# A fused gated layer with its backward pass on one core: sums of a short convolution moved to accumulating DMA, three more inverses in the wider form, forward products placed one step later

## The chip, the cores and the metric

The kernel runs on one core of a Trainium2 chip. The metric is the device time of one execution in microseconds; before the change the median of 3 runs is 1931.9 us (1931.69 to 1933.45). The profiled execution spans 1930.0 us, at a granted TensorE clock of 1.000.

## The reference, cut to what matters

The program computes one layer, its output and all its gradients (S = 2048 rows, D = 1024 channels, F = 3584, bf16):

```python
xn = layernorm(x)                                    # x: (S, D)
# A: a short convolution, a gate, a long convolution by FFT of length 2S
k_shift[s] = sum_t k[s - 3 + t] * shift_k[:, 3 - t]  # 4 taps, channel by channel
kv = k_shift * v
y  = irfft(rfft(kv, 2S) * rfft(ssm_k, 2S))[:S] + kv * ssm_D
s  = xn * y
# B: a bilinear gated unit
g  = silu(((xn @ w_gate) * (xn @ w_up)) @ w_down)
out = x + s * g
# and the gradients of x, k, v, shift_k, ssm_k, ssm_D, w_gate, w_up, w_down
```

## The kernel before, in words

The work runs in stages, and TensorE has matmuls in all of them. In the first, to about 521 us, xn is computed and multiplied with w_up and w_gate in 14 slabs of 256 columns. One unit of this (`gu_unit`) takes four blocks of 128 rows: 32 matmuls into PSUM tiles `psg` (line 661), ACT copies to `gut`, and one DVE multiply `hN` = gate x up, stored through the POOL queue (`Hd`), turned by TensorE some units later and stored as `HTd`. Then follow the product with w_down (`psbm`, line 985), the gates of the output, and the backward products (`psb`, `psx`).

The long convolution's forward half is a Python generator, `conv_forward`, that is pumped between the groups of `psg` matmuls: each `yield` gives the estimated cost of a step, and `tick` pulls steps so that the share of `F_TOTAL` that is done follows the share of the ticks that have passed. So the place of each step among the matmuls comes from these estimates. The DVE instructions of the generator, and the first matmul of each forward product, are pinned to this program order.

The 1024 channels are treated in eight slices (`ds`) of 128. For each slice there are two transforms, of the filter `h` together with `kv` pieces, into spectra KX and HX; then the product of the spectra; then an inverse transform. The steps, in order:

- `half` (lines 235 to 257): one half of a forward transform: 16 matmuls into two PSUM tiles `psF`, which ACT copies to an `SP` tile. There are two `SP` buffers and two `psF` buffers. Slices 0 and 7 use another form with eight residues (`EIGHT`).
- `transform`: the DVE sums of the two halves (`W<-SP`) and the outputs (`KX<-W`, `HX<-W`). At two places in it the function `ahead` issues the next half, or the turning of the next filter rows (`h_rows`).
- `product`: the spectra are multiplied on DVE, about 12 us.
- the inverse: `inv_dft` with four residues and four matmuls for each residue in the tail (`inv_rows`, line 449), or `inv8` with eight residues, more DVE work and two matmuls for each residue (`inv8_rows`, line 438). `INV8` says which slices take `inv8`: 2, 4 and 6. In the inverse the `kv` halves of the next slice are issued.

The short convolution (`shift`) makes `kv` for two slices (256 channels) at a time; `dp` counts these pairs. On DVE it is four products of `k` with a broadcast tap and three sums, all 128 x 4096 bf16, and a multiplication with `v`. `shift(0)` runs ahead of everything; those of `dp` 1, 2 and 3 (the "later shifts") run after the products of slices 1, 3 and 5. Their tiles are `krow` (k), `U[4]` (v), `U[6]` (the sum) and `U[7]` (the product of a tap). `load_kv` loads k and v for the next pair through the POOL queue; it is called at the start of slices 1, 3 and 5. `KFd`, `HFd`, `KSHd` and `YFd` are stores of the spectra, the shifted keys and the result, all on the POOL queue, which is in order.

The tiles `U[4]` to `U[7]` live in SBUF for the whole stage. After the last slice the generator ends, its PSUM is given back, and the `psbm` stage starts.

Of the kernel before, what the change touches and what calls it, by code (L numbers as in the profile page):

```python
# [13 lines left out]
BF16 = mybir.dt.bfloat16  # L14
# [5 lines left out]
def build_kernel(  # L20
# [11 lines left out]
    nc = tc.nc  # L32
    P = 128
# [3 lines left out]
    NB = S // P  # L37
# [206 lines left out]
    def net(w):  # L244
        w -= 0.95 * pe_us[0]
        pe_us[0] = 0.0
        return w
# [445 lines left out]

    h_out = []
    EIGHT = ((0, 0), (0, 1), (7, 0), (7, 1))
    INV8 = (2, 4, 6)
    SHIFT_W = 8 * 2.3

    conv_state = {"forward": True}
# [1 line left out]
    def conv_forward():  # L701
        S_ = conv_state

        def load_kv(dp, c):
            S_["k", dp] = krow
            if dp > 0 or c == 0:
                for i in range(2) if dp == 0 else (c,):
                    cld_k(krow[:, i], i, dp)
            if dp > 0 or c == 1:
                for i in range(2) if dp == 0 else (c,):  # L710
                    v = U[4][:, 2048 * i:2048 * i + 2048].rearrange("p (a x) -> p a x", a=8)
                    cld_v(v, i, dp * 256, 256)

        def load_h(ds):
            hrow = U[5][:, 0:2048].rearrange("p (c u r) -> p c u r", c=2, r=8)
            cld(U[5][:, 0:2048], A_ssm_k[ds * P:(ds + 1) * P, :])
            S_["h", ds] = hrow

        def shift(dp):
            kv = cx.tile([P, NB, 256], BF16, name="kv")  # L720
            S_["kvt", dp] = kv
            k = S_.pop(("k", dp))
            wb = lambda j: Wbc[:, j:j + 1, dp * 256:(dp + 1) * 256].unsqueeze(1).to_broadcast([P, 2, 8, 256])
            room = cx.tile([P, 16, 256], BF16, name="KX")[:].rearrange("p a x -> p (a x)") if dp == 0 else U[7][:]
            acc, prod, v = [t.rearrange("p (c r d) -> p c r d", c=2, r=8) for t in (U[6][:], room, U[4][:])]
            with tc.issue_after(last.ins):
                tt(acc, k[:, :, 0:8, :], wb(3), MUL)
            yield 2.3
            for j in (2, 1, 0):
                tt(prod, k[:, :, 3 - j:11 - j, :], wb(j), MUL)  # L730
                yield 2.3
                tt(acc, acc, prod, ADD)
                yield 2.3
            tt(kv[:].rearrange("p (c r) d -> p c r d", c=2), acc, v, MUL)
            st(KSHd[dp], U[6][:].rearrange("p (b d) -> p b d", b=NB))
            yield 2.3

        def h_rows(ds, c):
            if ds == 8:
                return  # L740
            hrow = S_["h", ds]
            if c == 0:
                S_["hx"] = cf.tile([P, NB, P], BF16, name="hx")
            pe_us[0] += 0.47
            ps = ps_tr.tile([P, 8, P], BF16, name="tr")
            with tc.issue_after(tr_ln[0].ins):
                nc.tensor.transpose(ps[:, 0, :], hrow[:, c, :, 0], ident[:])
            for r in range(1, 8):
                nc.tensor.transpose(ps[:, r, :], hrow[:, c, :, r], ident[:])
            nc.scalar.activation(S_["hx"][:, 8 * c:8 * c + 8, :], ps[:], ACT.Copy, scale=WSC)  # L750
            if c == 1:
                h_out.append(ds)
                if ds + 1 < 8:
                    load_h(ds + 1)

        def kvs(ds):
            return S_["kvt", ds // 2][:, :, ds % 2 * P:(ds % 2 + 1) * P]

        def tail(ds):
            G = S_.pop(("G", ds))  # L760
            yf = cs.tile([P, NB, P], BF16, name="yf")
            for rp in range(4):
                ps = (inv8_rows if ds in INV8 else inv_rows)(G, ps_y, rp)
                pe_us[0] += 0.45 if ds in INV8 else 0.9
                nc.scalar.copy(out=by_res(yf[:], rp), in_=rowps(ps))
                if rp == 3:
                    st(YFd[:, :, ds * P:(ds + 1) * P], yf[:])
                yield

        load_kv(0, 0)  # L770
        yield 0.0
        load_kv(0, 1)
        yield 0.0
        cx = pool("cx", 1)
        cs = pool("cs", 1)
        cf = pool("cf", 1)
        with tc.issue_after(xsts[3].ins):
            load_h(0)

        def half(ds, x, i, first=None):  # L780
            if (ds, int(first is not None)) not in EIGHT:
                return fwd4_half(x, i, cf, ps_cv, first)
            SP = cf.tile([P, 2, 2, 512], F32, name="SP", bufs=2)
            fwd8_half(x, i, SP, ps_cv, first, True)
            return SP

        def transform(ds, kind, sp, X, C, ahead, step):

            if (ds, kind) in EIGHT:
                W = fwd4_buf(cs)[:].rearrange("p a b c x -> p (a b c) x")  # L790
                for n, w in enumerate(fwd8(sp, X, W, C, ahead)):
                    if n in (0, 2, 4, 6):
                        step()
                    yield net(w)
                return
            W = fwd4_buf(cs)
            fwd4_sums(W, sp[0], 0)
            step()
            yield net(2.4)
            fwd4_sums(W, sp[1], 1)  # L800
            ahead(0)
            step()
            yield net(2.4)
            fwd4_outs(X, W, 0)
            ahead(1)
            step()
            yield net(2.4)
            fwd4_outs(X, W, 1)
            step()
            yield net(2.4)  # L810

        yield from shift(0)
        PIN[0] = True
        yield 3.9
        h_rows(0, 0)
        h_rows(0, 1)
        yield 0.1
        tl = turn_tables(ps_y)
        sp = [half(0, S_["hx"], i, Dz[:, 0:P]) for i in range(2)]
        for ds in range(8):  # L820
            yield 0.5
            if ds % 2 == 1 and ds < 7:
                with tc.issue_after(S_["kst"].ins):
                    for c in range(2):
                        load_kv(ds // 2 + 1, c)
            D0 = Dz[:, ds * P:(ds + 1) * P]
            sph = []
            KX = cx.tile([P, 16, 256], BF16, name="KX")
            HX = cs.tile([P, 16, 256], BF16, name="HX", bufs=2)
            own_room = lambda X: X[:].rearrange("p a x -> p (a x)").bitcast(F32).rearrange("p (a x) -> p a x", a=8)[:, 0:4]  # L830
            eight = (ds, 1) in EIGHT
            if ds == 0:
                yield from transform(0, 1, sp, HX, own_room(KX), lambda i: sph.append(half(0, kvs(0), i)), nop)
            else:
                yield from transform(ds, 0, sp, KX, own_room(HX), lambda i: sph.append(half(ds, S_["hx"], i, D0)), nop)
                S_["kst"] = st(KFd[ds], KX[:])
            next(tl, None)
            room = cf.tile([P, 4, 256], F32, name="room", tag="hx")[:] if eight else None
            yield from transform(ds, int(ds > 0), sph, HX if ds else KX, room, nop1 if eight else lambda c: h_rows(ds + 1, c),
                                 lambda: next(tl, None))  # L840
            if ds == 0:
                S_["kst"] = st(KFd[0], KX[:])
            if eight:
                h_rows(ds + 1, 0)
            turned(HX, 1, 0, 1)
            yield 1.3
            if eight:
                h_rows(ds + 1, 1)
            if ds == 7:
                cf.release()  # L850
                S_["forward"] = False
            st(HFd[ds], HX[:])
            yield from product(KX, HX, KX, cs, False, 0)
            if ds % 2 == 1 and ds < 7:
                yield from shift(ds // 2 + 1)
            sp = []

            def ahead():
                if ds < 7:
                    sp.append(half(ds + 1, kvs(ds + 1), len(sp)))  # L860
            yield from (inv8 if ds in INV8 else inv_dft)(KX, HX, cs, ahead if ds % 2 == 0 else None, ahead)
            if ds % 2 == 1:
                ahead()
            S_["G", ds] = HX
            tl = tail(ds)
        yield 6.0
        for _ in tl:
            yield 1.0
        cs.release()
        cx.release()  # L870
        kst.release()

    F_TOTAL = 4 * SHIFT_W + 6.0 + 8 * (0.5 + FWD4_W + 1.3 + PROD_W + INV_W) + 10.0 - 0.95 * 8 * (4 * 1.75 + 0.95 + 4 * 0.9)
    F_TOTAL += len(EIGHT) * (FWD8_W - 9.6 + 0.95 * 1.75) - 2.0
    F_TOTAL += len(INV8) * (INV8_W - INV_W + 0.95 * 1.8)
    conv = conv_forward()
# [771 lines left out]
```

## Time and profile before

| | PE | DVE | ACT | POOL | DMA share |
|---|---|---|---|---|---|
| whole span, 1930.0 us, busy us | 1913.8 | 1549.9 | 639.4 | 330.0 | |
| 120.7 to 480.4 us (slices 1 to 7), 359.7 us | 354.06 | 355.47 | 201.59 | 61.51 | 0.70 |
| 206 to 357 us, 151 us | 149.80 | 148.82 | 82.95 | 31.44 | 0.73 |
| 427 to 521 us, 94 us | 93.75 | 93.10 | 51.59 | 12.03 | 0.78 |

Each row is a stretch of the trace. A number is the time in which an engine had an instruction running. PE's ends are modelled, so its busy time says little of how densely it works; the start times of matmuls in the timeline are of more use. The DMA share is the mean share of the 16 DMA engines' time in which they had packets. A wait names the engine that waited, and the instruction that released it. The DMA table gives the time from issue to landing.

### The profile page before, as it was taken

How to read it: one execution, taken by the hardware profiler on the slowest of the kernel's cores; microseconds unless marked ns; L12 is line 12 of the kernel's file. 1: busy time of each engine (PE TensorE's matmuls, PEld its weight loads, DVE VectorE, ACT ScalarE, POOL GpSimd, SP SyncE). 2: the span in 40 equal slices, each digit the busy share in tenths (PEclk: the TensorE clock that was granted, in tenths of full speed). 3: DMA queues.
4: the chain of work that ended last, by engine and by line, in shares of the span. 5: the costliest groups of instructions: out<-in, count | busy, mean ns of one | idle time of the engine just before them, and what ended most of it. 6: DMA issues, size and time to landing. Idle time of an engine off the chain costs nothing.

```text
span 1930.0 us, 27487 instructions
## 1 busy us (share of the span) xinstructions
PE 1913.8 (99%) x10978; PEld 1030.2 (53%) x10978; DVE 1549.9 (80%) x1730; ACT 639.4 (33%) x942; POOL 330.0 (17%) x461
## 2 busy tenths in 40 slices
PE   8999999999999999999999999999999999999999
PEld 5555555555544457666666666664444444444444
DVE  9999999999937556888899999999996403388883
ACT  5764555555423234333222222221222102011113
POOL 4121212111112220000122132021111101111111
PEclk9999999999999999999999999999999999999999
DMA  8876766667889987666788788575797999889883
GB/s 292 268 259 217 254 211 228 225 199 265 283 252 316 310 284 264 211 206 207 262 247 262 243 238 269 195 268 186 219 258 172 141 215 218 163 179 193 194 204 130
DMA packets 451360, 444.43 MB, mean 230 GB/s; under 512 B 268800, under 2 KB 371612, under 8 KB 436768
## 3 DMA queue, kind: packets, MB, share of 16 engines
q1 hardware_dynamic: 394848, 243.36, 47.6%
q0 software_dynamic: 40064, 169.95, 27.3%
q10 hardware_dynamic: 16320, 29.36, 4.1%
q8 instruction: 86, 1.41, 0.3%
q14 instruction: 42, 0.34, 0.1%
HBM read 194.00 MB, written 185.64 MB: 197 GB/s over the span
## 4 chain that ended last, share of the span: by engine, by line
PE 85%; DVE 9%; issue 2%; DMA 2%; ACT 1%; SPq 0%; POOL 0%; ACTq 0%; DVEq 0%; POOLq 0%
PE psb L1356 20%; PE psx L1486 20%; PE psb L1339 10%; PE psbm L985 10%; PE psg L661 10%; PE psb L1434 9%; DVE W L213 2%; PE psF L235 2%; DVE HX L213 1%; DVE KX L213 1%; DVE U L213 1%; PE psY L438 1%; DMA HTd<-hT 1%; PE psY L1132 1%; DVE bst L561 1%
## 5 line engine op out<-in xcount | busy, mean ns | idle before, releaser
L661 PE MATMUL psg<-wslab,U 128*128 128x512 bf16 x1792 | 407.3, 379 | 2.9 <-DMA wslab<-in_B_w_gate_dram 0.9
L1356 PE MATMUL psb<-U,U 128*128 128x512 bf16 x1792 | 397.0, 379 | 0.0
L1486 PE MATMUL psx<-U,dgut 128*128 128x512 bf16 x1536 | 332.8, 379 | 0.0
L1486 PEld LDWEIGHTS <-dgut 128*128 128x128 bf16 x1792 | 175.3, 98 | 211.4
L1356 PEld LDWEIGHTS <-U 128*128 128x128 bf16 x1792 | 175.3, 98 | 197.9
L661 PEld LDWEIGHTS <-U 128*128 128x128 bf16 x1792 | 172.6, 98 | 188.9 <-issue 2.1
L1339 PE MATMUL psb<-wdt,U 128*128 128x256 bf16 x1792 | 205.6, 273 | 0.0
L1339 PEld LDWEIGHTS <-U 128*128 128x128 bf16 x1792 | 175.2, 98 | 29.2
L1434 PE MATMUL psb<-U,U 128*128 128x512 bf16 x816 | 177.1, 379 | 0.0
L213 DVE TENSOR_TENSOR W<-W 128x1024 f32<-128x1024 f32 (+1 forms) x174 | 171.6, 1003 | 3.7
L1361 ACT CAST wb<-psb 128x512 bf16<-128x512 f32 x112 | 65.6, 586 | 315.1 <-PE psb L1356 304.7
L985 PE MATMUL psbm<-U,ht 128*128 128x512 bf16 x672 | 145.7, 379 | 0.0
L1434 PEld LDWEIGHTS <-U 128*128 128x128 bf16 x896 | 87.4, 98 | 104.5
L663 ACT CAST gut<-psg 128x512 bf16<-128x512 f32 x156 | 91.5, 587 | 127.8 <-PE psg L661 127.0
L1518 ACT ACTIVATE dx_t<-dxn 128x1024 bf16<-128x1024 f32 x15 | 15.9, 1058 | 324.9 <-DVE dxn L213 321.0
L985 PEld LDWEIGHTS <-ht 128*128 128x128 bf16 x672 | 65.6, 98 | 78.6
L213 DVE TENSOR_TENSOR U<-U,dht 128x2048 bf16<-128x2048 bf16 x56 | 68.3, 1221 | 46.9 <-ACT dht L1341 46.9
L1184 DVE SCALAR_TENSOR_TENSOR dkp<-dkT,kT 128x1024 bf16<-128x1024 bf16 (+2 forms) x64 | 78.4, 1224 | 33.3 <-DMA dkT<-DKSHd 31.5
L1341 ACT CAST dht<-psb 128x512 bf16<-128x512 f32 x112 | 65.7, 587 | 116.3 <-PE psb L1339 116.3
L213 DVE TENSOR_TENSOR dxn<-psx,dxna_t 128x1024 f32<-128x1024 f32 x15 | 18.3, 1222 | 83.3 <-PE psx L1486 79.2
L66 POOL DMA_DIRECT2D Hd<-hN x54 | 37.0, 685 | 265.7 <-DVE hN L213 263.9
L1465 ACT CAST wbs<-psb 128x512 bf16<-128x512 f32 x51 | 29.9, 586 | 146.5 <-PE psb L1434 134.2
(260 smaller groups left out, 2462.8 us busy)
## 6 DMA issues: line engine op xcount, KB each, us to landing
U<-GUd SPq DMA_DIRECT2D x28, 1024.0 KB, 7.7
DGd<-U SPq DMA_DIRECT2D x28, 1024.0 KB, 5.9
GUd<-gut ACTq DMA_DIRECT2D x39, 512.0 KB, 5.1
out_dram<-wb SPq DMA_DIRECT2D x112, 128.0 KB, 4.1
U<-Hd SPq DMA_DIRECT2D x14, 1024.0 KB, 5.9
Hd<-hN POOLq DMA_DIRECT2D x54, 256.0 KB, 4.5
HTd<-hT SPq DMA_DIRECT2D x52, 256.0 KB, 3.7
ht<-HTd SPq DMA_DIRECT2D x6, 1536.0 KB, 10.1
```

What stands on the lines that cost most here:

```text
L213: pinned(V.tensor_tensor(o, a, b, op))
L235: mm = nc.tensor.matmul(ps[:, k].rearrange("p (c d) -> p c d", c=2), T[:, r, k, :], xr[:, r], start=(n == 0), stop=(n == len(rs) - 1 and ( ...
L661: gu_mm[0] = nc.tensor.matmul(ps[:], XNT[q][:, dc, qi * P:(qi + 1) * P], w[:, dc].rearrange("p a f -> p (a f)"), start=(dc == 0), stop=(dc ...
L663: nc.scalar.copy(out=gut[:, :, i], in_=ps[:].rearrange("p (a f) -> p a f", a=2))
L985: mm = nc.tensor.matmul(ps[:, dh * 512:(dh + 1) * 512], ht(fc)[:, i * P:(i + 1) * P], WD[fc // 4][:, fc % 4, dh * 512:(dh + 1) * 512], sta ...
L1184: ins = V.scalar_tensor_tensor(prod[:].rearrange("p r d -> p (r d)")[:, lo:H], dkT[:, 0, lo:H], 1.0, kT[:, 0, 13 + m + lo:13 + m + H], op0 ...
L1339: nc.tensor.matmul(ps[:, x * SLW:(x + 1) * SLW], DBMT[2 * hf + g][:, dc, (b % 4) * P:(b % 4 + 1) * P], wdt[:, dc, :], start=(dc == 0), sto ...
L1341: nc.scalar.copy(out=dht[:, 2 * e:2 * e + 2].rearrange("p b f -> p (b f)"), in_=ps[:])
L1356: nc.tensor.matmul(ps[:], XN[b // 4][:, b % 4, dc * P:(dc + 1) * P], dgus[b // 8][:, :, b % 8], start=(b == 0), stop=(b == NB - 1))
L1361: nc.scalar.copy(out=wb[:, dc % 2].rearrange("p a f -> p (a f)"), in_=ps[:])
L1434: nc.tensor.matmul(ps, h[:, f, b, :], DBM[b // 4][:, b % 4, dh * 512:(dh + 1) * 512], start=(b == 0), stop=(b == NB - 1))
L1486: nc.tensor.matmul(ps[:, dh * 512:(dh + 1) * 512], t[n][:, f, i * P:(i + 1) * P], WGU[n][:, f, dh * 512:(dh + 1) * 512], start=(n == 0 and ...
```

## The change

It has four parts.

1. The three sums of each later shift are no longer DVE instructions. `shift_parts` computes the product of a tap on DVE into `U[7]`, and an accumulating DMA on the POOL queue adds it to `U[6]`. As the product tile is used again, each product must wait until the DMA before has landed; so the three parts are spread over the slice: two products ahead of the first transform, one after it, one after the second transform, and the multiplication with v after the product of the spectra. `shift(0)` stays as it was.
2. `INV8` takes in slices 1, 3 and 5, so six inverses use the form with eight residues.
3. In `transform` (the form of slices 1 to 6) both calls of `ahead` come one step later.
4. The loads of k and v for the next pair are issued at the end of the even slice before, since the first product is now needed at the start of the odd slice. `F_TOTAL` is adapted to the new sum of costs.

It is for taking work off DVE and spending it on inverses that need fewer matmuls, and for giving the forward products more distance from the sums that free their buffers.

```diff
-    INV8 = (2, 4, 6)
+    INV8 = (1, 2, 3, 4, 5, 6)
...
+        def shift_parts(dp):
+            k = S_.pop(("k", dp))
+            wb = lambda j: Wbc[:, j:j + 1, dp * 256:(dp + 1) * 256].unsqueeze(1).to_broadcast([P, 2, 8, 256])
+            rows = lambda t: t.rearrange("p (c r d) -> p c r d", c=2, r=8)
+            acc, prod, v = rows(U[6][:]), rows(U[7][:]), rows(U[4][:])
+            def part(j):
+                tt(prod, k[:, :, 3 - j:11 - j, :], wb(j), MUL)
+                pinned_add = nc.gpsimd.dma_start(out=U[6][:], in_=U[7][:], accum_op=ADD, max_dma_last_dim=4096)
+                return pinned_add
+            tt(acc, k[:, :, 0:8, :], wb(3), MUL)
+            yield 2.3
+            part(2)
+            yield 2.3
+            yield None
+            for j in (1, 0):
+                part(j)
+                yield 2.3
+                yield None
+            kv = cx.tile([P, NB, 256], BF16, name="kv")
+            S_["kvt", dp] = kv
+            tt(kv[:].rearrange("p (c r) d -> p c r d", c=2), acc, v, MUL)
+            st(KSHd[dp], U[6][:].rearrange("p (b d) -> p b d", b=NB))
+            yield 2.3
...
             fwd4_sums(W, sp[1], 1)
+            step()
+            yield net(2.4)
+            fwd4_outs(X, W, 0)
             ahead(0)
             step()
             yield net(2.4)
-            fwd4_outs(X, W, 0)
+            fwd4_outs(X, W, 1)
             ahead(1)
-            step()
-            yield net(2.4)
-            fwd4_outs(X, W, 1)
             step()
             yield net(2.4)
...
+            sh = iter(())
             if ds % 2 == 1 and ds < 7:
-                with tc.issue_after(S_["kst"].ins):
-                    for c in range(2):
-                        load_kv(ds // 2 + 1, c)
+                sh = shift_parts(ds // 2 + 1)
+            def some():
+                for w in sh:
+                    if w is None:
+                        return
+                    yield w
+            yield from some()
...
                 S_["kst"] = st(KFd[ds], KX[:])
+                yield from some()
...
             st(HFd[ds], HX[:])
+            yield from some()
             yield from product(KX, HX, KX, cs, False, 0)
-            if ds % 2 == 1 and ds < 7:
-                yield from shift(ds // 2 + 1)
+            yield from some()
+            if ds % 2 == 0 and ds < 6:
+                with tc.issue_after(S_["kst"].ins):
+                    for c in range(2):
+                        load_kv(ds // 2 + 1, c)
...
-    F_TOTAL = 4 * SHIFT_W + 6.0 + 8 * (0.5 + FWD4_W + 1.3 + PROD_W + INV_W) + ...
+    F_TOTAL = SHIFT_W + 3 * 5 * 2.3 + 6.0 + 8 * (0.5 + FWD4_W + 1.3 + PROD_W + INV_W) + ...
```

More of the change, by code (lines that the diff above doesn't have):

```diff
@@ L871, in conv_forward @@
         kst.release()
-    F_TOTAL = 4 * SHIFT_W + 6.0 + 8 * (0.5 + FWD4_W + 1.3 + PROD_W + INV_W) + 10.0 - 0.95 * 8 * (4 * 1.75 + 0.95 + 4 * 0.9)
+    F_TOTAL = SHIFT_W + 3 * 5 * 2.3 + 6.0 + 8 * (0.5 + FWD4_W + 1.3 + PROD_W + INV_W) + 10.0 - 0.95 * 8 * (4 * 1.75 + 0.95 + 4 * 0.9)
     F_TOTAL += len(EIGHT) * (FWD8_W - 9.6 + 0.95 * 1.75) - 2.0
```

## The prediction

> **What bounds the kernel now.** I read the stage table (40 windows), then the waits of each engine between 90 and 530 us, then the timelines of DVE, PE and ACT there, because the change touches only the forward stage, which ends near 530 us. Two rows of the stage table, each: window, length, then busy us (instructions) of PE, weight loads, DVE, ACT and POOL, granted clock, DMA share, GB/s:
>
> ```profile
> 386.00:434.25 48.25, 47.44 (x296) 26.68 (x295) 47.84 (x36) 26.43 (x37) 5.20 (x8) 1.00 0.60 199
> 530.75:579.00 48.25, 48.25 (x241) 23.41 (x240) 14.61 (x24) 12.80 (x14) 6.21 (x9) 1.00 0.87 251
> ```
>
> In the forward stage DVE and TensorE are both full at 99%; from 530 us on TensorE is full and DVE has room. TensorE then stays full until about 1880 us, so what the forward stage saves or loses on TensorE moves the end one to one. The page's "99% PE" does not say which of the two sets the pace here; the waits and the timelines do. Waits of PE (first line) and of DVE (the others) from 90 to 530 us, in us in total, times, longest:
>
> ```profile
> PE psF L235 <- ACT SP L257: 4.9, 4, 2.5
> DVE hN L213 <- ACT gut L663: 0.8, 1, 0.8
> DVE W L213 <- ACT gut L663: 0.5, 1, 0.5
> ```
>
> Each engine waits for the other a little: TensorE waits 4.9 us in four places, DVE 1.3 us in two. One of the four places, on PE, ACT and DVE (start, length):
>
> ```profile
> 426.36 1.95 PE L235 MATMUL psF<-hx,TF 128*128 128x256 bf16 x16 [0.80 <-ACT SP L257]
> 425.29 1.93 ACT L257 COPY SP<-psF 128x1024 f32<-128x1024 f32 x2 [1.10 <-DVE W L213]
> 422.82 4.63 DVE L213 TENSOR_TENSOR W<-SP 128x1024 f32<-128x1024 f32 x4
> ```
>
> A forward product (psF) needs its PSUM buffer, which the ACT copy of the half before empties, which needs an SP buffer (two of them), which the DVE sums of two halves earlier free. So the second half can start only about 1.1 us after the DVE sums of three halves earlier. DVE has no gap around there. These products, last at 479.3 us, are where a late DVE stops TensorE; after the last one nothing in DVE holds TensorE.
>
> **What the skill says.** (1) "Collectives: The Full Stack", section "The bandwidth ceiling: the fold count and why AG ≠ RS ≠ AR": an adding transfer is slower than a copy because it reads two sources for each write, not because of the add; reduce-scatter measured 32.35 GB/s against 62.28, on two engines, so some 16 GB/s for one engine. The trace has no accumulating DMA, so no run here shows it yet. (2) "DMA: Bandwidth & Descriptors", section "SWDGE vs HWDGE vs iDMA": accumulation goes through GpSimd's queue only. So the new transfers stand in the queue with the KFd, HFd and Hd stores. (3) "SBUF — State Buffer", "Who interferes with whom": a tensor_tensor with both inputs in SBUF contends with GpSimd's reads, and (an inference, it says) not with descriptor writing. The trace agrees: POOL issues a 1 MB KFd store in 557 ns while DVE is 99% busy.
>
> **The change, part by part.**
>
> *TensorE work.* Inverses 1, 3 and 5 go from four matmuls for each residue to two: 16 fewer each, 48 in all. Eight such matmuls take 0.87 us start to start (431.17 to 432.04 in the timeline), 0.109 us each: 5.2 us less TensorE work.
>
> *DVE work.* Rows by shape (busy us, mean ns):
>
> ```profile
> L213 DVE TENSOR_TENSOR U<-U,U 128x4096 bf16<-128x4096 bf16 x9 | 20.6, 2289 | 0.2
> L213 DVE TENSOR_TENSOR U<-k,Wbc 128x4096 bf16<-128x4096 bf16 x12 | 27.3, 2286 | 0.1
> ```
>
> The nine sums U<-U,U go to the DMA. Start to start such an instruction costs 2.27 us (a whole shift from 165.08 to 184.40 less two hN multiplies of 0.60: 18.1 us for eight), so 20.4 us go. The three wider inverses cost more: an eight-residue inverse takes 456.03 to 473.07 less two hN, 15.8 us; a four-residue one 412.84 to 422.82 less one hN, 9.4; 6.4 more each, 19.3 in all. Net about -1 us; counted instruction by instruction at the last forward product it is -0.7. So the DVE work is traded, not reduced; only TensorE gets lighter.
>
> *Forward products one step later, new total of the pump.* Nothing is added; it changes where the products stand among the gate matmuls. I counted, in both built orders, TensorE work and DVE work ahead of every half. For the last half (filter product of slice 7, second half) 1624 gate matmuls stand before it, then 1627. TensorE work ahead of it falls by 4.5 us, that behind it by only 0.7. For the same half of slice 6 the split is 0.9 ahead and 4.3 behind.
>
> *Loads of k and v one step earlier.* Their place in the POOL order for the first of them (slice 1) does not change: the second block of k is issued at 124.69 us and its 704 KB take 8.7 us, landing at 133.4. The first product of the shift now stands ahead of slice 1's transform, where DVE arrives at 131.8 us. That is a new DVE wait of 1.6 us. For slices 3 and 5 an eight-residue inverse lies between, and the loads land well ahead: nothing.
>
> *The nine accumulating DMAs.* New waits of DVE: the next product overwrites U7, so it waits until the DMA has read it, and the last multiply waits for U6. Queued behind a waiting DVE instruction is everything on DVE in order: transform sums (TensorE's products wait for these), hN multiplies. The room for each is what DVE does between, from slice 1 of the trace before: KX transform with one hN 131.80 to 141.07 plus 0.6, 9.9 us; HX transform and turn 141.07 to 152.09, 11.0; product with two hN 152.09 to 165.08, 13.0. For the duration, plain 1 MB stores of the same queue land so (KB each, median us):
>
> ```profile
> KFd<-KX POOLq DMA_DIRECT2D x8, 1024.0 KB, 4.6
> HFd<-HX POOLq DMA_DIRECT2D x8, 1024.0 KB, 5.9
> KSHd<-U POOLq DMA_DIRECT2D x3, 1024.0 KB, 5.2
> ```
>
> From below: about 2 us of fixed time (the Trainium skill, "DMA: Bandwidth & Descriptors", section "Anatomy of one DMA — SWDGE (gpsimd) path") and 1.05 MB at 16 engines x 16 GB/s, 4.1 us, is 6.1 us, an estimate from the collectives figures. From above: moving twice, in engines that are already 0.55 to 0.95 busy in these windows, and behind a KFd or HFd store issued 2.3 us ahead: with what that store still needs (up to 3.6 us) and twice the movement of a slow HFd (8.2 us landing, so twice 6.2), some 14 to 16 us. I take 7 for the first, 9 for the second (2.3 us behind KFd), 10 for the third: all below 9.9, 11.0 and 13.0, so no stall. The spread keeps both ends.
>
> *Sum.* The end follows DVE's path to the last forward product. DVE reaches the sums that free it 0.7 us earlier by work, 1.2 earlier because its waits on gut go (TensorE is ahead now); the half had 2.8 us of slack before (479.3 against 475.4 + 1.1); the TensorE work behind it is 0.7 less. Together 5.4 us, less the 1.6 us of the k load: 3.8. 1931.9 - 3.8 = 1928.1. The same sum at slice 6's half gives 4.3 + 0.7 + 0.7 + 1.2 = 6.9 less 1.6, so it doesn't bind. I say 1928.0.
>
> **The rivals.**
> A, TensorE alone sets the pace: the later products leave enough slack that a late DVE is never seen. Then all 5.2 us and the 4.9 us of waits go: about 1921.8. For it: only four waits. Against: DVE is 99% busy and its work is not less.
> B, slower: the accumulations become the bound. At 12 us each the stalls are 2.1 + 1.0 + 0 per slice, 9.3 over three: 1937.4. At 15 us 5.1 + 4.0 + 2.0, 33 in all: 1961. For it: DMA share 0.94 in the window 152 to 165 of the trace and an unmeasured operation. Against: the estimate of 6 to 10 us.
> C, the accumulations cost about what is won: 10.5 to 11.5 us each, some 0.6 to 2.1 us per slice, 2 to 6 in all: 1930 to 1934.
>
> **How the numbers follow.** The forecast (1926 to 1929.5) 0.40, A 0.15, C 0.22, B 0.23. Faster by over 0.2% is below 1928.04: A whole, and some two thirds of the forecast, since the k wait may be partly hidden: 0.15 + 0.28 = 0.43. Slower is above 1935.76: B but for its mildest part and none of C, 0.22. The rest, 0.35, is no change. Range 1922.5 (A's region nearly whole) to 1941 (the milder half of B): some 0.07 below and 0.12 above left out.
>
> **What would show it.** PE's waits on SP between 90 and 530 us near 3 to 5 us still, not 0 (A). DVE waits on k of about 1.6 us near 132 us. DVE waits on the U DMA of under 1 us each in nine places; over 2 us shows B. The accumulating DMA's landing in the DMA table: 7 to 10 us. The first psbm matmul (520.97 us before) near 517. The prediction is wrong if the accumulations land later than 11 us, if ACT's hT copies start to wait for HTd stores (0.2 us before) because the DMA engines are fuller, or if the stages after 530 us change at all.

## The result, and the profile after

The changed kernel takes 1940.12 us (median of 4 runs, 1939.49 to 1940.28), the kernel before 1931.98 (4 runs); the ratio is 1.004, 95% interval 1.0023 to 1.0057. It is some 8 us slower, where 4 us less were forecast. The profiled execution spans 1938.2 us.

The stage table again, for the same two stretches; the columns are those of before (window, length, then busy us and instructions of PE, weight loads, DVE, ACT and POOL, granted clock, DMA share, GB/s):

```profile
386.00:434.25 48.25, 42.94 (x236) 21.98 (x239) 43.51 (x41) 21.00 (x31) 7.52 (x10) 0.93 0.86 263
530.75:579.00 48.25, 47.96 (x247) 23.81 (x251) 21.08 (x27) 13.80 (x16) 4.76 (x7) 1.00 0.86 246
```

In the forward stage TensorE lost 4.5 us of 48 and DVE 4.3, the granted clock fell to 0.93, and the DMA share rose from 0.60 to 0.86. From 530 us on TensorE is as full as before (all of that stage lies 8.2 us later, so the window holds a little other work). The first `psbm` matmul starts at 529.16 us (520.97 before), and from there to the end both kernels take 1409.0 us, so the whole loss, 8.2 us, is there when the forward stage ends.

What is as planned shows in the rows by shape of DVE and in the DMA table (KB each, median us to landing). No sum `U<-U,U` of this shape is left, the nine accumulating DMAs have taken their place, and only the waits ahead of the rows are new (x13 counts the whole execution, with one product of the first shift):

```profile
L213 DVE TENSOR_TENSOR U<-k,Wbc 128x4096 bf16<-128x4096 bf16 x13 | 29.6, 2287 | 1.6 <-DMA k<-in_A_k_dram 1.6
L213 DVE TENSOR_TENSOR kv<-U,U 128x4096 bf16<-128x4096 bf16 x4 | 9.2, 2292 | 6.9 <-DMA U<-U 6.9
```

```profile
HTd<-hT SPq DMA_DIRECT2D x52, 256.0 KB, 4.1
U<-U POOLq DMA_DIRECT2D x9, 1024.0 KB, 9.8
HFd<-HX POOLq DMA_DIRECT2D x8, 1024.0 KB, 7.8
```

The median landing of 9.8 us lies in the forecast 7 to 10, but it hides two kinds. By slice (1, 3, 5) the first accumulation took 8.0, 8.4 and 8.5 us, the second 9.8, 10.0 and 8.7, the third 14.2, 15.3 and 15.1.

The waits from 90 to 545 us, in us in total, times, longest: PE, then DVE, then ACT (its ordinary waits on PE and DVE left out).

```profile
PE psg L661 <- ACT gut L663: 9.2, 2, 4.9
PE psF L235 <- ACT SP L257: 2.0, 1, 2.0
...
DVE kv L213 <- DMA U<-U: 6.9, 3, 2.7
DVE W L213 <- ACT SP L257: 2.7, 2, 1.7
DVE U L213 <- DMA k<-in_A_k_dram: 1.6, 1, 1.6
...
ACT hT L691 <- DMA HTd<-hT: 14.7, 3, 6.6
```

Three of these are new and large. DVE waits 6.9 us for the third accumulations; ACT waits 14.7 us for `HTd` stores (0.2 before); TensorE waits 9.2 us for ACT in two places, where it waited for none of ACT's `gut` copies before. The timelines of the second place, of SP's queue, ACT and PE (start, length, instruction, idle time before it and its releaser), show how the last two hang together:

```profile
387.42 0.37 SPq L540 DMA_DIRECT2D wslab<-in_B_w_up_dram  x1
387.84 1.89 SPq L540 DMA_DIRECT2D wslab<-in_B_w_gate_dram  x1
392.40 21.77 SPq L61 DMA_DIRECT2D HTd<-hT  x3
...
412.78 1.01 ACT L691 COPY hT<-tr 128x1024 bf16<-128x1024 bf16 x1 [6.61 <-DMA HTd<-hT]
413.69 1.08 ACT L663 CAST gut<-psg 128x512 bf16<-128x512 f32 x2
...
407.77 1.67 PE L661 MATMUL psg<-wslab,U 128*128 128x512 bf16 x7
414.33 2.29 PE L661 MATMUL psg<-wslab,U 128*128 128x512 bf16 x5 [4.88 <-ACT gut L663]
```

The slab loads issued at 387 us land only after 11.8 and 24.2 us. The `HTd` store of 392.40 stands behind them in SP's queue and lands after 20.3. There are two `hT` buffers and a copy into one of them every 7.35 us (391.36 and 398.71 us), so a store that takes more than some 13.6 us (two such steps less the copy of 1.0) holds up a copy: the next copy `hT<-tr` on ACT waits until 412.7; the `gut` casts stand behind it in ACT's order; and TensorE, out of `psg` buffers, idles for 4.88 us. The other place is the same at 298.30 us (4.28 us idle). The Trainium skill ("DMA: Bandwidth & Descriptors", section "Queues, rings and completion order") says that SP's queue has one ring on each engine and that each engine takes the descriptors of a ring in order; the store that lands 0.6 us after the slab load ahead of it (412.7 and 412.1) agrees.

The idle time has a tail. The columns of these windows are those of the stage table:

```profile
142.00:146.00 4.00, 4.00 (x20) 2.48 (x20) 4.00 (x4) 2.73 (x3) 0.00 (x0) 0.57 1.02 195
...
406.00:410.00 4.00, 3.45 (x16) 1.47 (x15) 2.22 (x3) 0.17 (x1) 0.00 (x0) 1.00 1.05 248
410.00:414.00 4.00, 0.00 (x0) 0.00 (x0) 3.23 (x2) 1.22 (x2) 1.25 (x2) 0.76 1.08 418
414.00:418.00 4.00, 3.45 (x8) 1.28 (x9) 3.93 (x4) 0.83 (x3) 0.00 (x0) 0.50 0.94 362
418.00:422.00 4.00, 4.00 (x30) 2.60 (x29) 3.97 (x6) 2.29 (x4) 0.69 (x1) 0.89 0.21 73
```

After the idle 4.88 us the granted clock is 0.50 for some 4 us and 0.89 in the 4 after: 4 x 0.50 + 4 x 0.11, 2.4 us of TensorE time more. The Trainium skill ("TensorE: Matmul & The Clock Gate", section "Part 1: The HAM clock gate") gives the clock as halved after an idle window of some 3.4 us and restored after as long a busy one; both stalls, of 4.28 and 4.88 us, agree. But here a shorter gap did it too: the 2.0 us that a `psF` product waits at 140 us are followed by a clock of 0.57 from 142 to 146 us, 1.7 us more, while the longest `psF` wait before the change, 2.5 us, left the clock at 1.00. So the two stalls take 4.3 + 4.9 + 2 x 2.4, about 14 us, from TensorE in this execution; how much of this reaches the end the experiments had to tell. The DMA share is over 1 (the times of packets overlap) from 406 to 414, up to the landings, and 0.21 after.

### The profile page after: what moved, and what is told of

Read it like the earlier page. It is cut to its first block, busy times and chain, and to the rows that moved or that the text cites. A ratio compares the mean times of both kernels' runs of the same rounds, so it can differ in the third digit from the quotient of the medians.

```text
span 1938.2 us, 27286 instructions
## 1 busy us (share of the span) xinstructions
PE 1906.9 (98%) x10796; PEld 1027.8 (53%) x10930; DVE 1547.1 (80%) x1751; ACT 637.8 (33%) x942; POOL 341.8 (18%) x470
## 4 chain that ended last, share of the span: by engine, by line
PE 83%; DVE 5%; issue 3%; DMA 3%; ACT 1%; POOL 1%; POOLq 0%; ACTq 0%; DVEq 0%
PE psb L1393 20%; PE psx L1523 20%; PE psb L1376 10%; PE psbm L1022 10%; PE psb L1471 9%; PE psg L661 8%; DMA HTd<-hT 2%; DVE W L213 2%; PE psF L235 2%; PE psY L438 1%; DVE KX L213 1%; PE psY L1169 1%; DMA U<-U 1%; PE psx L1471 1%; DVE m L213 1%
## 5 line engine op out<-in xcount | busy, mean ns | idle before, releaser
L213 DVE TENSOR_TENSOR W<-W 128x1024 f32<-128x1024 f32 (+1 forms) x192 | 190.1, 1007 | 4.1
```

The source lines that it names most:

```text
L213: pinned(V.tensor_tensor(o, a, b, op))
```

## The experiments

My theory after this reading: the intended parts are worth about what was forecast, and two losses eat it, the waits for the third accumulation on DVE's path and the `HTd` stall on TensorE's. The rivals: that the later products or the wider inverses cost the time; that the size of the packets, not the amount of data, delays the other transfers. All ratios, to the kernel before run beside each (they are not quotients of two medians; where kernels of different experiments are compared below, it is by these ratios):

| kernel | us | ratio | 95% interval |
|---|---|---|---|
| after | 1940.12 | 1.0040 | 1.0023 to 1.0057 |
| e1 copies in place of sums | 1930.07 | 0.9988 | 0.9981 to 0.9994 |
| e2 third sum on DVE | 1936.56 | 1.0025 | 1.0017 to 1.0034 |
| e3 inverses as before | 1945.91 | 1.0069 | 1.0054 to 1.0084 |
| e4 forward products as before | 1941.44 | 1.0051 | 1.0033 to 1.0070 |
| e5 HTd stores on ACT's queue | 1936.08 | 1.0018 | 1.0004 to 1.0033 |
| e6 smaller packets | 1948.44 | 1.0090 | 1.0074 to 1.0105 |
| e7 all nine sums on DVE | 1947.31 | 1.0079 | 1.0064 to 1.0094 |
| e9 three mends | 1930.57 | 0.9986 | 0.9975 to 0.9998 |
| e10 three mends, five wide inverses | 1928.02 | 0.9975 | 0.9968 to 0.9982 |
| e11 kv multiply later | 1938.70 | 1.0037 | 1.0022 to 1.0052 |
| e12 before, products one step later | 1931.21 | 0.9997 | 0.9981 to 1.0013 |
| e13 e5 and e11 together | 1929.68 | 0.9987 | 0.9979 to 0.9995 |
| e14 three mends, four wide inverses | 1932.48 | 1.0004 | 0.9996 to 1.0012 |

### e1: the change without the adding

```diff
-  nc.gpsimd.dma_start(out=U[6][:], in_=U[7][:], accum_op=ADD, max_dma_last_dim=4096)
+  nc.gpsimd.dma_start(out=U[6][:], in_=U[7][:], max_dma_last_dim=4096)
```

The transfers stay, with their order and waits, but copy instead of adding; the later shifts' sums are left out.

> The nine accumulating DMAs become plain copies of the same megabyte at the same places; the sums of the later shifts are left out, so k_shift is wrong for 768 channels, and nothing else changes. Theory (the adding transfers hold the DMA engines about twice as long as a copy, the SP queue starves, HTd stores land late, ACT waits for hT and TensorE for ACT): landing of U<-U falls from 9.8 us to 5 to 7, the DVE wait of kv from 6.9 us to under 1, the ACT wait of hT from 14.7 us to under 2, TensorE's waits on gut from 9.2 to 0; time 1925 to 1930 us. Rival 1 (any further megabyte in this queue does it): waits and time stay, 1936 to 1940. Rival 2 (the loss is in the wider inverses or in the place of the forward products): time stays near 1940.

Measured: 1930.07 us, ratio 0.9988. The largest wait of PE:

```profile
PE psF L235 <- ACT SP L257: 4.6, 4, 2.5
```

The copies land in 6.1 us (median). DVE does not wait for the third transfer and TensorE does not stall behind `HTd`; DVE's wait for k stays, 1.5 us. So everything in the change but the adding brings -2.3 us (-3.7 to -1.2), and adding instead of copying costs 0.9988 to 1.0040, 10 us.

### e7: the sums on DVE at the new places

```diff
-  nc.gpsimd.dma_start(out=U[6][:], in_=U[7][:], accum_op=ADD, max_dma_last_dim=4096)
+  tt(acc, acc, prod, ADD)
```

> All nine sums go back to DVE, at the places of the parts; six wide inverses and the later products stay. DVE has 20.4 us more work and no waits on U. Theory that DVE's path to the last product sets the end here: 1928 + 20 less what the 2 to 3 us of slack take, 1943 to 1949 us. Rival (DVE has room that the profile does not show): 1930 to 1936 us.

Measured: 1947.31, ratio 1.0079; TensorE's `psF` products wait 12.0 us:

```profile
PE psF L235 <- ACT SP L257: 12.0, 5, 3.7
```

Against e1 this is 17.6 us for 20.4 us of DVE sums: DVE's path to the forward products does set the end, as the forecast had it.

### e8: what an accumulating DMA takes by itself

A kernel that computes nothing of the layer: 1 MB accumulations, copies and stores one at a time, then slab loads of the same shape alone and beside them. It ran once.

```diff
+  for f in (lambda: add(4096), copy, store, lambda: add(1024)):
+      for i in range(4):
+          fresh(False)
+          f()
+  ...            # slab loads alone, then each of the three with slab loads
```

> Nothing of the layer is computed: only transfers of one megabyte, one at a time, then each beside a slab load of two times 512 KB that starts with it on SP's queue. In order: four accumulations in rows of 4 KB, four plain SBUF copies, four stores to HBM, four accumulations in rows of 1 KB; three slab loads alone; then three slab loads beside each of accumulation 4 KB, copy, accumulation 1 KB. Theory: alone an accumulation lands in 6 to 9 us, a copy in 4 to 5.5, so an accumulation moves data at about half the rate; beside an accumulation of 4 KB rows the slab load takes 3 to 6 us longer than alone, beside a copy 1 to 3 us, beside 1 KB rows less than beside 4 KB. Rival (the add costs as much as a copy): accumulation and copy within 1 us.

Measured, from issue to landing: accumulation 7.9 to 8.0 us, copy inside SBUF 4.6 to 4.7, store 4.1 to 4.2, accumulation in rows of 1 KB 8.8 to 8.9 (three accumulations of the four: the first had another transfer beside it). The answers for the tile of the sum: the first two lines stand for the accumulations, the next two for the copies.

```profile
L53 POOL DMA_DIRECT2D acc<-prod x3: 1192/1192/1197, 23.6 to 49.5; - x3
DMA to landing us min/median/max: 7.9/7.9/8.0
...
L56 POOL DMA_DIRECT2D acc<-prod x4: 713/718/742, 62.4 to 91.2; - x4
DMA to landing us min/median/max: 4.6/4.6/4.7
```

So an accumulation takes 1.7 times a copy. The forecast's estimate from below, 6.1, is too low by 1.8 us with idle engines already. The two slab loads alone land in 4.0 and 5.2 us; issued 3 us behind an accumulation in 7.8 and 9.0, and then the accumulation takes 8.9; issued together with one in 4.0 and 5.6, and then the accumulation takes 10.7. That last part missed my expectation: in these two cases, one of each, who is first takes the less harm. Neither of them makes 15 or 24 us; what else in the real stage does was not taken apart.

### e6: is it the packets?

```diff
-  ... accum_op=ADD, max_dma_last_dim=4096)
+  ... accum_op=ADD, max_dma_last_dim=1024)
```

> The accumulating DMAs are cut into rows of 512 elements (1 KB) instead of 2048 (4 KB), nine times the same bytes. Theory that [...]big adding packets starve the small packets of SP's slab loads: with small packets the slab loads and HTd stores land earlier (HTd under 12 us, slab under 15), the accumulations land later (12 to 20 us) and the DVE waits grow; hT waits under 5 us; time 1934 to 1945 us with the loss in DVE waits instead. Rival (only the amount of data counts): HTd stores as late as in the changed kernel, near 20 us at 280 and 400 us.

Measured: 1948.44, ratio 1.009; the landing rises to 10.8 us, the waits of `kv` to 15.1, of `hT` to 20.2, and the latest `HTd` store lands after 22.5 us. Large packets that hold up the loads are not the cause: with small ones all of it grew. That fits the time for which the accumulation keeps the engines, which is longer in small rows (8.9 against 7.9 alone) and shorter for the copies of e1.

### e2: two accumulations for each shift instead of three

```diff
+  if j == 0:
+      tt(acc, acc, prod, ADD)
+      return
   nc.gpsimd.dma_start(out=U[6][:], in_=U[7][:], accum_op=ADD, max_dma_last_dim=4096)
```

> The third sum of each later shift, whose transfers took 14 to 15 us, goes back to DVE, the first two stay on the DMA. Theory: DVE gets 3 x 2.27 = 6.8 us of work and loses 6.9 us of waits on kv, the HTd stores near 280 and 400 us land in under 12 us, TensorE's waits on gut go; time 1926 to 1931 us. Rival (the loss comes from DVE, which is full): no gain, 1938 to 1942.

Measured: 1936.56, ratio 1.0025, a miss: only 2.9 us better than after. The `kv` waits are gone and TensorE's stalls shrink to 0.8 and 2.5 us, but three sums are 6.8 us on DVE, and DVE sets the end: against e1 the kernel is 7.1 us longer. My expectation let the 6.9 us of waits that go pay for the sums, and counted the end of the stall on top; but the two losses seem to be worth less together than one by one (e13).

### e3 and e4: the wider inverses and the later products, each taken back

```diff
-    INV8 = (1, 2, 3, 4, 5, 6)
+    INV8 = (2, 4, 6)
```

> Only slices 2, 4 and 6 take the inverse with eight residues, as before the change; the rest is as changed. TensorE has 5.2 us more, DVE 19.3 us less. Theory (DMA congestion stops ACT and TensorE): hT waits of over 10 us and waits on gut stay, as the order of transfers is much the same; 1937 to 1945 us. Rival (DVE is what is short): 1926 to 1932 us.

Measured: 1945.91, ratio 1.0069, slightly above my upper end. Waits of PE and DVE:

```profile
PE psg L661 <- ACT gut L663: 14.2, 4, 5.0
...
DVE hN L213 <- ACT U L663: 22.5, 6, 5.8
```

DVE, with 19.3 us less to do, now waits for ACT 22.5 us, and the kernel is 5.6 us slower than after: TensorE has the 5.2 us of matmuls that were counted, and its stall is longer (14.2 us against 9.2). How the 5.6 us divide between these is not shown. The wider inverses are not what costs.

```diff
   fwd4_sums(W, sp[1], 1)
+  ahead(0)
   step()
   yield net(2.4)
   fwd4_outs(X, W, 0)
-  ahead(0)
+  ahead(1)
   step()
   yield net(2.4)
   fwd4_outs(X, W, 1)
-  ahead(1)
```

> The forward products stand where they stood before the change; the rest is as changed. Theory: the loss stays, with more waits on psF: 1939 to 1945 us. Rival (the later products starve DVE of its inputs, it waited 2.7 us for SP): under 1936 us.

Measured: 1941.44, ratio 1.0051, not distinguishable from after, with both kinds of waits still there (`kv` 3.9, `hT` 13.7, `psg` 7.4 us). That the later products cost something is not seen; the two intervals would hide some 5 us.

### e12: the later products alone, in the kernel before

The edit is the third part of the change, in the kernel before.

> The kernel before with one part of the change alone, the forward products one step later. My forecast's step gave these and the new total of the pump up to 2.8 + 1.2 us of slack where TensorE waits 4.9 us: psF waits 2 to 5 us and a time of 1928 to 1931, ratio 0.998 to 0.9995. Rival: DVE sets the end at slice 7 whatever the place of the products: 1931 to 1933, no difference.

Measured: 1931.21, ratio 0.9997 (0.9981 to 1.0013): no gain that the times can tell, though the median lies 2.1 us under that of the kernel before beside it (1933.30). The trace tells more: the first `psbm` starts at 518.96 us, 2.0 us earlier than before, and a single late wait, for which the kernel before has no counterpart, takes it back in this execution:

```profile
518.96 3.62 PE L985 MATMUL psbm<-U,U 128*128 128x512 bf16 x16
...
PE psx L1486 <- DVE dxn L213: 1.9, 1, 1.9
```

The gain of 4.0 us from more slack (2.8 + 1.2), which the forecast counted, would be 0.9979 and lies just outside the interval. The test is a partial one: neither the lighter inverses nor the pump's new total are in this kernel.

### e5: HTd stores off SP's queue

```diff
-  ld(HTd[b0 // 8][sl // 12][fr:fr + SLW, ...        # SP's queue
+  sta(HTd[b0 // 8][sl // 12][fr:fr + SLW, ...       # ACT's queue
```

> All HTd stores are issued on ACT's DMA queue instead of SP's, so that they no longer stand behind the two slab loads there; the accumulations stay. Theory (what stops ACT is the HTd store queued behind slab loads that starve in the SP queue): landing of HTd under 8 us everywhere, hT waits under 3 us, TensorE's waits on gut under 1; the kv waits of about 7 us stay; some 50 further DMA issues of 0.5 us on ACT; time 1928 to 1934 us. Rival (the DMA engines as a whole are late, whatever the queue): HTd lands late here too, 1938 to 1943.

Measured: 1936.08, ratio 1.0018, between the two ranges. Waits of PE and DVE from 90 to 545 us:

```profile
PE psF L235 <- ACT SP L257: 7.8, 4, 2.9
...
DVE kv L213 <- DMA U<-U: 5.0, 3, 2.1
```

No `hT` copy waits for a store any more, and no `psg` matmul for ACT. The stores land after 13.2 us at most, not under 8 as I had it, but within the 13.6 us that two buffers allow, while a slab load beside them takes 26.1: the queue is what held them. What is left is DVE's path: 5.0 us for the third accumulations, and the `psF` products that wait for it. A third `hT` buffer, another mend for the stall, was not tried.

### e11 and e13: the multiplication with v later, without and with e5

```diff
   yield from product(KX, HX, KX, cs, False, 0)
-  yield from some()
 ...
-  yield from (inv8 if ds in INV8 else inv_dft)(KX, HX, cs, ...)
+  for n, w in enumerate((inv8 if ds in INV8 else inv_dft)(KX, HX, cs, ...)):
+      yield w
+      if n == 1:
+          yield from some()
```

The third accumulation gets two steps of the inverse, 4.7 us of DVE work, more.

> The changed kernel with only the multiplication with v placed later. My theory: the kv waits (6.9 us) go to under 1.5, and with them what DVE's path loses, while the hT waits on HTd stay near 12 to 15: 1935 to 1937.5, ratio 1.0015 to 1.003. Rival: after the stall of TensorE DVE has slack, so the kv waits are hidden behind it: 1939 to 1941 as after.

Measured: 1938.70, ratio 1.0037. No `kv` multiply waits for a DMA, and yet the 0.6 us against after cannot be told from nothing: 1938.70 lies between the two ranges, nearer the rival's. PE stalls as in after, and DVE now waits for ACT instead (4.5 us). PE's wait, and the clock behind its two stalls (columns of the stage table):

```profile
PE psg L661 <- ACT gut L663: 9.1, 2, 4.9
...
296.00:300.00 4.00, 3.77 (x15) 1.67 (x15) 4.00 (x6) 1.13 (x3) 0.69 (x1) 0.62 0.90 351
...
410.00:414.00 4.00, 2.38 (x6) 0.95 (x7) 4.00 (x6) 1.84 (x3) 0.69 (x1) 0.71 1.01 396
414.00:418.00 4.00, 4.00 (x28) 2.40 (x27) 3.93 (x5) 1.85 (x3) 0.00 (x0) 0.86 0.43 156
```

The profiled execution is the fastest of the eleven, 1936.48 us, and reaches `psbm` 3.5 us before after's. Most of this is the clock: its stalls are as long (4.24 and 4.87 us), but behind them it loses 4 x 0.38, 1.5, and 4 x (0.29 + 0.14), 1.7 us, where after's lost 2.4 and 2.4, and 1.7 more at 142 us. So the tail of a stall is not a fixed price, and part of the spread between executions is this.

> The changed kernel with two of the three mends: HTd stores on ACT's queue and the multiplication with v later; the loads of k and v as in after. Against e9_three_mends (0.9986) it has only the old order of these loads. My theory: the losses are not a sum, the later multiplication is worth nothing alone (e11_kv_later) because TensorE's stall is longer, but about 5 us once the HTd stall is gone; the k load is worth its 1 us: ratio 0.9988 to 0.9998, k wait 1.5, kv waits under 1.5. Rival: the 1.6 us k wait at slice 1, early in the stage, shifts everything behind it into worse places, and it was the larger part of the gain of e9: ratio 1.0008 to 1.0018.

Measured: 1929.68, ratio 0.9987, though the third accumulations land hardly sooner than in after (12.9, 14.7 and 14.6 us). What the `psF` products wait for:

```profile
PE psF L235 <- DVE kv L213: 3.7, 2, 1.9
PE psF L235 <- ACT SP L257: 2.5, 1, 2.5
```

So it is not how fast the accumulations land, but who must wait for them. The four kernels make a square:

| | kv multiply as in after | later |
|---|---|---|
| HTd on SP's queue | 1.0040 | 1.0037 |
| HTd on ACT's queue | 1.0018 | 0.9987 |

The stall alone costs 1.0037 - 0.9987, 9.7 us; the `kv` waits alone 1.0018 - 0.9987, 6.0 us; both together 10.2, near the larger and not the sum. By the four intervals each of these is good to some 3 us, and the 5.5 us by which the sum exceeds the whole to some 5.5: that both losses are real is shown, that they overlap is likely. The timeline has a way for it: at 410 us DVE waits for the accumulation (408.2 to 410.8) just ahead of and into TensorE's wait for ACT (409.5 to 414.3), and while TensorE is stopped a late DVE holds up nobody. What the move of the `HTd` stores does in a kernel without a stall was not run; the square takes it as nothing.

### e9, e10 and e14: both mends, the k loads first, and how many wide inverses

```diff
   with tc.issue_after(S_["kst"].ins):
+      S_["k", ds // 2 + 1] = krow
       for c in range(2):
-          load_kv(ds // 2 + 1, c)
+          cld_k(krow[:, c], c, ds // 2 + 1)
+      for c in range(2):
+          cld_v(...)
-    INV8 = (1, 2, 3, 4, 5, 6)
+    INV8 = (2, 3, 4, 5, 6)       # e10; (2, 3, 4, 6) in e14
```

> The changed kernel with three mends: HTd stores on ACT's DMA queue, both blocks of k loaded ahead of v, and the multiplication with v that follows the third accumulation placed 4.7 us of DVE work later (inside the inverse, after its second step). My theory: after loses 4.2 us by late HTd stores and some 5.8 us on DVE's path, 5.0 of it waits for the third accumulation and 1.6 the k load; with all three gone it comes to the kernel with plain copies or 1 us above it, 1929 to 1932.5, ratio 0.999 to 1.0005; kv waits 0 to 1, k wait 0 to 0.5, no hT waits on HTd. Rival: the accumulations cost through the general fullness of the DMA engines, whatever the order: the waits move elsewhere (to HX sums, slab loads or the second accumulation) and the time stays at 1934 to 1938.

Measured: 1930.57, ratio 0.9986, equal to e13 and to the copies of e1. The k wait falls from 1.6 to 0.6 us; whether the time follows these runs can't tell, with intervals of 2.3 us (e9) and 1.5 us (e13) either way.

> As e9_three_mends, but slice 1's inverse in the four-residue form again (INV8 without 1): 6.4 us less DVE work, 1.7 us more TensorE work. If DVE's path to the last forward product sets the end (psF waits of 4 to 5 us with plain copies), up to 4.6 us of waits go and 1.7 come: 1926.5 to 1930, ratio 0.997 to 0.999, psF waits under 3. Rival: TensorE sets the end already: 1.7 us slower than e9_three_mends, 1931 to 1934.

Measured: 1928.02, ratio 0.9975, faster than both kernels; the first `psbm` starts at 515.86 us. Waits of PE and of DVE:

```profile
PE psF L235 <- DVE kv L213: 4.2, 2, 2.9
...
DVE W L213 <- ACT SP L257: 2.9, 1, 2.9
```

The waits for the `SP` copies are nearly gone (0.2 us, 1.4 in e9), those for `kv` are not, so `psF` waits 4.4 us and not under 3; DVE begins to wait for TensorE's side, 5.4 us in all. The step from e9 is 2.1 us, with intervals that overlap; that e10 beats before does not depend on it.

> As e10_mends_inv5 with slice 5's inverse in the four-residue form too (INV8 2, 3, 4, 6): another 6.4 us less on DVE, 1.7 us more on TensorE. In e10 the waits are already mutual (PE 4.4, DVE 5.4 us), so my theory is that TensorE sets the end from here on: the psF waits fall under 2.5 and the time is 0 to 1.7 us above that of e10, ratio 0.9975 to 0.9985. Rival: DVE still sets the end: psF waits fall and the time with them by 1.5 to 2.5 us, ratio 0.996 to 0.9968.

Measured: 1932.48, ratio 1.0004, 5.6 us more than e10, and neither theory had that: one gave 1.7 us more, the other 2 less. Of the 5.6, 1.7 are TensorE's additional matmuls. PE's waits rise from 4.4 to 6.8 us, 2.4 more. DVE's largest:

```profile
DVE hN L213 <- ACT gut L663: 6.1, 6, 1.9
DVE W L213 <- ACT SP L257: 5.4, 3, 3.9
```

DVE idles 14.2 us while TensorE still waits for it elsewhere: the order in which the pump weaves the steps seems to fit this split of work less well. The rest is the clock, at least in the profiled executions: behind a `psF` wait of 2.6 us it is 0.58 from 185 to 189 us, 1.7 us, where e10's is 1.00 throughout. Why the order fits worse stays open.

## Why the prediction was wrong

**TensorE's work, -5.2 us.** Not contradicted, but not measured by itself: taking the three wide inverses back cost 5.6 us (e3), with a stall that was 5.0 us longer too. With the stall mended, one wide inverse less cost nothing (e10).

**DVE's work, traded and not reduced; DVE's path sets the end.** Right. The nine sums are worth 17.6 of the 20.4 us counted (e7 against e1), and where the accumulations hold nobody (e1, e9, e13) `psF` waits for DVE are still there, 4.6 to 6.3 us, near the 3 to 5 us that were named (in e9 and e13 most of it for the `kv` multiply that was moved). Rival A, which has them gone, is out.

**The k load, 1.6 us.** Its size was exact: 1.6 us of DVE wait at slice 1. Its cost stays open: loading k first took 1.0 us of the wait away (e9 against e13), and a gain of that size is below what these runs can tell. I added a wait on an early slice to the end as if nothing between had slack, and gave no reason.

**Later products and slack, 4.0 of the 5.4 us.** Seen at most in part: alone the later products bring TensorE 2.0 us by the end of the forward stage (e12, one trace) and nothing that the times can tell, and taking them back from the change costs nothing that can be told (e4). All intended parts together bring 2.3 us, against 3.8 forecast, and 3.8 lies just outside e1's interval (-3.7 to -1.2). The sum was of the right size; which of its terms is too large is not shown.

**The nine accumulations, no stall.** This step failed, by a term that was too small. It took 7, 9 and 10 us against room of 9.9, 11.0 and 13.0. The first two came at 8.0 to 8.5 and 8.7 to 10.0, and waited nowhere. The third came at 14.2 to 15.3, the "some 14 to 16 us" of the estimate from above, and DVE waited 1.6 to 2.7 us for it each time. The estimate from below started from 6.1 us where the operation alone takes 7.9, and at slice 5 the third one has two slab loads, a filter load, the YFd and HFd stores and two Hd stores around it, at a DMA share over 1. The copies of e1 at that place took 9.2, 11.8 and 10.2 us, against 4.7 to 5.1 at the first: the place is slow for any transfer, and the adding makes 14 to 15 of it. Rival B's own third term, (15 - 13.0) x 3, is 6 us; as the only loss it measured 6.0, give or take 3 (e5 against e13). So B was right for one third of the transfers, and its 1961 for all nine was far off.

**The HTd stores.** The text said that the prediction is wrong "if ACT's hT copies start to wait for HTd stores", and gave this neither a time nor a place in the range: a term put at nothing without a reason. Alone it costs 9.7 us (e11 against e13), the larger of the two losses. The forecast costed a new transfer by who waits for it and by what it waits for, not by the transfers that pass the same engines later: two slab loads in SP's queue, the store behind them, ACT's order behind that, and a clock at half speed after the idle.

Together: -2.3 us from what the change is for, and 10.2 us from the adding, where the two losses seem to overlap. That 1940.1 lies within the stated 1922.5 to 1941 is luck: the upper part stood for rival B's stalls, and those of the first and second accumulations did not come, while the `HTd` stall was in no rival.

## What to carry to other kernels

An asynchronous operation that takes work off a full engine has to be costed three times: for the one that waits for it, for its own time beside the traffic of that very stretch (here 15 us where it takes 7.9 alone), and for the other transfers that it delays, followed through their queue to an engine that works in order. Take a consumer of such a transfer to the latest place that the data allows, and keep small stores that free buffers out of a queue in which bulk loads stand. Two losses that stall different engines at the same time need not add, so mending the smaller one alone may show little (0.6 us for the `kv` waits here, 6.0 once the stall was gone, each to some 3 us or more).

## What the runs showed of the hardware

- A 1 MB accumulation inside SBUF takes 7.9 us with nothing else, a plain copy of the same tiles 4.6, a store 4.1; POOL needs 1.19 us to issue it, against 0.72 and 0.54. In rows of 1 KB it takes 8.9 us and 1.55 to issue.
- Of an accumulation and slab loads the one issued first suffered less, in one case of each (e8): loads 3 us behind land in 7.8 and 9.0 us instead of 4.0 and 5.2, and the accumulation takes 8.9 instead of 7.9; issued together the loads lose 0.4 at most, and the accumulation takes 10.7.
- A stall of 4.2 to 4.9 us on TensorE is followed by a stretch at a granted clock of 0.50, which costs 2.4 us on top in after and 1.5 and 1.7 in e11. A wait of 2 to 3 us can do the same, 1.7 us (2.0 us in after, 2.6 in e14), and need not (2.5 us before, 2.9 in e10).
- A 256 KB store behind two slab loads in SP's queue lands after 19.7 and 20.3 us (after); from ACT's queue, beside the same loads, after 13.2 at most (e5).
